# Key-value sums in five blocks instead of eight, and another order of VectorE's work in the value steps

## The chip, the cores and the metric

The kernel runs on one core of one Trainium2 chip. The metric is the device time of one execution in microseconds; lower is better. The time before is a median of 554.52 us over three runs (554.31 to 555.47).

## The reference, cut to what matters

A transformer block without a causal mask: a linear-attention layer and a token-mixing MLP, each after a layer norm, each with a residual. S = 2048 rows, D = 1024, 32 heads of 32. The change lies in the first half of the attention layer.

```python
h = layernorm(x)                                  # 2048 x 1024
q, k, v = split(h @ wqkv)                         # 32 heads of 32
phi = lambda t: where(t > 0, t + 1, exp(t)) + 1e-6
pq, pk = phi(q), phi(k)
kv = einsum("bhsd,bhse->bhde", pk, v)             # one 32 x 32 matrix per head, summed over all rows
z = einsum("bhsd->bhd", pk)
o = (pq @ kv) / (pq @ z + 1e-6)                   # then @ wo, the residual and the MLP
```

## The kernel before

The rows are worked in 16 tiles of 128, and from tile 2 on in pairs: pair q holds tiles 2q and 2q + 1. Each row tile is loaded (`load_x`), gets its statistics on VectorE (`ln_stats`), is normalised (`ln_finish`: two small ScalarE operations for `rstd`, one VectorE `tensor_scalar`, then a DMA transpose on the sync queue into `xnT`). The transposed rows are the matmuls' stationary operand.

Keys and values of a pair are two 256-row projections. Each is done by a Strassen-like scheme with seven products instead of eight (class `Run`, methods `p1` to `p7`). A product is four matmuls of 512 columns. The products need sums of blocks of the weights (`w_sums`, made once) and of the rows (`x_sums`, four VectorE subtractions or additions for each pair, into `xs`). The results are built up in three running PSUM tiles: `psA`, `psB`, `psC`, and `psE` for `p5`. ScalarE copies `psA` to `psB` and `psB` to `psC` between products. Two of the four output blocks are read by VectorE with an addition of `psE`'s copy (`add`, after `p7` from `psC` and after `p3` from `psB`); the two others are read by ScalarE (`evac`, after `p2` and `p4`). `p4` goes on accumulating in `psC` after the addition has read it.

A key step (`KRun`) sends its results through the feature map `phi`: ScalarE makes exp and relu, VectorE a `tensor_scalar` (line 190) and an addition (line 194), into a key buffer `pk`. A value step (`VRun`) writes its results into a value buffer `vaug`, which has a 33rd column of ones in every head, so that the sum over keys comes out with the matrix. `QRun` does the same for part of the queries, into `pqT`.

`run_step(n, prev, ...)` writes one step by hand, in program order (`pin`). It overlaps two runs: it issues `n.p1`, `prev.p3`, `prev.p4`, `n.p6`, `n.p2`, `n.p5`, `n.p7`, and between them the VectorE parts of both (`dve11` ... `dve22`: the four feature maps of a key pair) and callbacks (`after6`, `after5`, `after7`). Each engine runs its own instructions strictly in that order. The loop goes over q = 2 to 7 with a key step and a value step for each (K2, V2, K3, V3, ...); at q = 5 a query step follows each of them, and two query steps and the rest of the query projections follow the loop.

`kv_accum(i)` adds tile i to the key-value sums: 32 small matmuls, one for each head, with a stationary operand of 128 x 32 and a moving operand of 128 x 33. Four of them stand side by side in TensorE's columns (`tile_position`). It is called for two tiles at a time: tiles 0 and 1 before the loop, tiles 2q - 2 and 2q - 1 in every value step between `p5` and `p7`, and tiles 14 and 15 after the loop. That makes eight blocks of 64 matmuls. Keys and values stand in rings of four buffers each (`NPK`, `NVA`), which is two pairs.

In a value step before, VectorE's order from the statistics on is: the second feature map of the key step before it (`dve12`), the normalisation of a coming tile (`ln_finish` in `after5`), the addition after `p7`, the four sums for the next pair (`x_sums` in `after7`).

Of the kernel before, what the change touches and what calls it, by code (L numbers as in the profile page):

```python
# [10 lines left out]
P = 128  # L11
F32 = mybir.dt.float32
BF16 = mybir.dt.bfloat16
# [17 lines left out]
def kernel(  # L31
# [15 lines left out]
    S, D = x.shape  # L47
# [187 lines left out]
    class Inner:  # L235
        banks = 4
        behind = None
# [185 lines left out]
    class Mixer1(Product7):  # L423
# [27 lines left out]
        def finish(self):  # L451
            while self.todo:
                e = self.todo.pop(0)
                dve.tensor_tensor(e[:, CW:D], e[:, CW:D], e[:, 0:CW], ALU.subtract)
# [324 lines left out]
    with ExitStack() as actx:  # L779
# [13 lines left out]
        pqT = pqpool.tile([P, ND, S], BF16)  # L793
# [15 lines left out]
        with ExitStack() as a1:  # L809
            e1pool = a1.enter_context(tc.tile_pool(name="e1pool", bufs=1))  # L810
            epool = a1.enter_context(tc.tile_pool(name="epool", bufs=2))
            a1w = a1.enter_context(tc.tile_pool(name="a1w", bufs=1))
            wkv = a1w.tile([P, ND, 2 * D], BF16)
            NVA, NPK = 4, 4
            vaugs = [a1w.tile([P, ND * HB, DH + 1], BF16, name=f"vaug{t}") for t in range(NVA)]
            for t in range(NVA):
                nc.vector.memset(vaugs[t][:, :, DH:DH + 1], 1.0)
# [3 lines left out]

            def by_head(t):
                return t.rearrange("p (h e) -> p h e", e=DH)
            pks = [a1w.tile([P, D], BF16, name=f"pk{t}") for t in range(NPK)]
            tv = [
                t.bitcast(FP16).rearrange("p (k c) -> p k c", c=CW)
                for t in (wo_sb[:, 2 * t:2 * t + 2, :].rearrange("p a b -> p (a b)") for t in range(4))
# [50 lines left out]
            def ln_stats(i):  # L878
                ln[i] = ln_chunks(i, xs.pop(i))
                for c in range(NDC):  # L880
                    pin(ln[i][1](c))
                pin(ln[i][2]())

            def ln_finish(i):
                xn, _, _, scale, norm, _, _ = ln.pop(i)
                for op in scale():
                    pin(op)
                pin(norm(slice(0, D)))
                nc.sync.dma_start_transpose(out=xnT[:, :, i * P:(i + 1) * P], in_=xn[:])
# [29 lines left out]
            def kv_accum(i):  # L919
                for j in range(ND):  # L920
                    for q in range(HB):
                        h = j * HB + q
                        pin(nc.tensor.matmul(
                            kv_ps[q * DH:(q + 1) * DH, j, :],
                            lhsT=pks[i % NPK][:, h * DH:(h + 1) * DH],
                            rhs=vaugs[i % NVA][:, h, :],
                            start=False,
                            stop=(i == NS - 1),
                            skip_group_check=True,
                            tile_position=(0, q * DH),  # L930
                        ))

            hk2 = ND // 2

# [9 lines left out]
            def w_sums(mov, part):  # L944
                (b11, b12, b21, b22), (t1, t2, t3, t4) = mov
                for out, a, b in ((t1, b12, b11), (t2, b22, t1), (t3, b22, b12), (t4, b21, t2))[part]:
                    pin(nc.vector.tensor_tensor(out, a, b, ALU.subtract))
# [3 lines left out]
            def x_blocks(q):  # L951
                v = xnT[:, :, q * 2 * P:(q + 1) * 2 * P].rearrange("p (k two) (h f) -> p k two h f", two=2, h=2)
                return v[:, :, 0, 0, :], v[:, :, 1, 0, :], v[:, :, 0, 1, :], v[:, :, 1, 1, :]

            def x_sums(q, part=slice(0, 4), home=None):
                a11, a12, a21, a22 = x_blocks(q)
                s1, s2, s3, s4 = [xs_sb[:, q % 2, t] for t in range(4)] if home is None else home[q % 2]
                for out, a, b, op in (
                    (s1, a21, a22, ALU.add), (s2, s1, a11, ALU.subtract),
                    (s3, a11, a21, ALU.subtract), (s4, a12, s2, ALU.subtract),  # L960
                )[part]:
                    pin(nc.vector.tensor_tensor(out, a, b, op))  # L962
# [164 lines left out]
            def run_step(n, prev, after6=None, after5=None, after7=None, fill=None, after3=None):  # L1127
                if n is not None:
                    n.p1()
                else:  # L1130
                    fill()
                prev.late22()
                prev.p3()
                if after3 is not None:
                    after3()
                prev.dve22()
                prev.p4()
                if n is not None:
                    n.p6()
                prev.dve21()  # L1140
                if after6 is not None:
                    after6()
                if n is not None:
                    n.p2()
                    n.p5()
                prev.late12()
                if n is not None:
                    n.dve11()
                behind = QRun in (type(n), type(prev))
                if not behind:  # L1150
                    prev.dve12()
                if after5 is not None:
                    after5()
                if n is not None:
                    n.p7()
                if behind:
                    prev.dve12()
                if after7 is not None:
                    after7()
# [159 lines left out]
            NVP = NS // 2  # L1319
# [5 lines left out]
            def load_next(i):  # L1325
                if i < NS:
                    xs[i] = load_x(i)

            v1 = VRun(1)
            v1.p1()  # L1330
            q_fill()
            kv_accum(0)
            kv_accum(1)
            v1.p6()
            v1.p2()
# [9 lines left out]
            prev = v1  # L1345
# [3 lines left out]
            for q in range(2, NVP):  # L1349
                runs = [KRun(q), VRun(q)]  # L1350
                if q == 5:
                    runs = [runs[0], QRun(q // 2, 0), runs[1], QRun(q // 2, 1)]
                for n in runs:
                    kind = type(n).__name__[0]
                    i = {"K": 2 * q + 3, "V": 2 * q + 4}.get(kind, NS)
                    if q == 5 and kind == "Q":
                        i = NS - 1 if n.half == 1 else NS
                    elif q == 6 and kind == "K":
                        i = NS

                    def after6():
                        if i < NS:
                            ln_stats(i)

                    def after5():
                        if kind == "V":
                            kv_accum(2 * q - 2)
                            kv_accum(2 * q - 1)
                        if i < NS:
                            ln_finish(i)  # L1370
                            load_next(i + 2)

                    def after7():
                        if kind == "V" and q != 5 and q + 1 < NVP:
                            x_sums(q + 1)
                        if kind == "Q" and n.half == 1:
                            x_sums(q + 1, slice(0, 3))
                        if kind == "K" and q in q_sums:
                            w_sums(qmov, q_sums[q])
                        for x in late_sums.get((kind, q), ()):  # L1380
                            x_sums(x[0], x[1], late_parts)

                    def after3():
                        if type(prev) is QRun and prev.half == 1:
                            x_sums(q, slice(3, 4))

                    run_step(n, prev, after6, after5, after7, after3=after3)
                    prev = n
            r1, r2 = (QRun(1, half, late_home) for half in range(2))
# [3 lines left out]
            def last_accum():  # L1393
                kv_accum(NS - 2)
                kv_accum(NS - 1)

            run_step(r1, prev)
            run_step(r2, r1, after6=last_accum)
            run_step(None, r2, fill=q_fill)
            q_fill()  # L1400
# [472 lines left out]
```

## Time and profile before

| what | value |
|---|---|
| median of 3 runs (lowest, highest) | 554.52 us (554.31, 555.47) |
| the profiled execution, its span | 554.72 us, 553.0 us |
| PE busy | 546.5 us (99%), 3867 matmuls |
| DVE (VectorE) busy | 450.5 us (81%) |
| ACT (ScalarE) busy | 290.3 us (52%) |
| granted TensorE clock | 1.00 |
| small matmuls `kvps<-vaug,pk` | 512, first and last start at 33.6 and 140.9 us |

PE is TensorE's matmuls and PEld its weight loads, which overlap them; DVE is VectorE, ACT ScalarE, SP the sync queue. A row of the profile names the line of the code, the operation, what it writes and reads, and a bracket with the idle time before it and what ended it. Matmuls are pipelined, so that one's busy time runs into the next; how fast TensorE goes is read from the differences of the starts.

### The profile page before, as it was taken

To read this page: it belongs to the slowest core of one execution; us is meant where nothing else is said; L and a number is where in the kernel's file an instruction comes from. 1 tells how busy PE (TensorE), PEld (TensorE's weight loads), DVE (VectorE), ACT (ScalarE), POOL (GpSimd) and SP (SyncE) were. 2 spreads that over 40 slices of the span, in tenths; PEclk is the share of its full clock that TensorE was granted. 3 is DMA by queue.
4 is the path that set the end of the run, shared out by engine and by line. 5 is a ranking of instruction groups with operands and counts; after the bars stand their busy time and mean duration, and the time that the engine had idled before them with its cause. 6 is when DMAs were issued, how large, how long until landed. Compare 5 with 4: busy or idle time off the path is not lost.

```text
span 553.0 us, 9926 instructions
## 1 busy us (share of the span) xinstructions
PE 546.5 (99%) x3867; PEld 320.3 (58%) x3867; DVE 450.5 (81%) x875; ACT 290.3 (52%) x616; POOL 26.3 (5%) x36
## 2 busy tenths in 40 slices
PE   8999999999999999999999999999999999999997
PEld 3444446646634444456666766766445667667665
DVE  7798888765886999889988889888986979749747
ACT  5748768676788777636556465564210413413310
POOL 1000000000000000000000000000002103103111
PEclk9999999999999999999999999999999999999999
DMA  9933341205636991104041340422868749849334
GB/s 291 319 78 77 77 85 32 40 1 153 229 106 171 303 317 76 58 0 152 4 153 52 101 152 2 152 60 76 229 213 206 211 135 242 210 140 220 90 107 75
DMA packets 83087, 74.58 MB, mean 135 GB/s; under 512 B 15826, under 2 KB 74464, under 8 KB 83040
## 3 DMA queue, kind: packets, MB, share of 16 engines
q1 hardware_dynamic: 78656, 69.87, 42.5%
q0 software_dynamic: 4096, 3.68, 4.8%
q8 instruction: 30, 0.49, 0.4%
q10 hardware_dynamic: 288, 0.39, 0.2%
q14 instruction: 17, 0.14, 0.1%
HBM read 59.12 MB, written 11.67 MB: 128 GB/s over the span
## 4 chain that ended last, share of the span: by engine, by line
PE 96%; DMA 2%; DVE 1%; ACT 0%; issue 0%; SPq 0%; DVEq 0%; ACTq 0%
PE psI L230 26%; PE psC L230 16%; PE acc_t L230 13%; PE psB L230 8%; PE psC L973 4%; PE psB L973 4%; PE psA L973 4%; PE acc_t L893 3%; PE psB L342 2%; PE psA L342 2%; PE psE L973 2%; PE psC L342 2%; DMA wkv<-in_A_wqkv_dram 2%; PE acc_t L1308 2%; PE psA L1107 1%; PE psC L1107 1%
## 5 line engine op out<-in xcount | busy, mean ns | idle before, releaser
L230 PEld LDWEIGHTS <-is 128*128 128x128 f16 x736 | 71.9, 98 | 31.1 <-DVE hi L230 0.4
L230 PEld LDWEIGHTS <-sa 128*128 128x128 f16 x606 | 59.3, 98 | 27.1
L230 PEld LDWEIGHTS <-wq 128*128 128x128 bf16 (+1 forms) x496 | 48.5, 98 | 28.1 <-issue 1.0
L230 PE MATMUL acc_t<-wo_sb,pqT 128*128 128x512 f16 x256 | 55.6, 379 | 0.0
L487 POOL DMA_DIRECT2D out_dram<-wq x28 | 24.4, 935 | 514.6 <-DVE sa L334 395.7
L230 PEld LDWEIGHTS <-pqT 128*128 128x128 bf16 x256 | 25.0, 98 | 30.5 <-issue 0.6
L230 DVE TENSOR_TENSOR t<-psI,t 128x256 f32<-128x256 f32 (+1 forms) x45 | 20.8, 475 | 22.2 <-PE psI L230 20.9
L230 PE MATMUL psC<-gs,wq 128*128 128x512 f16 x140 | 34.1, 379 | 0.0
L973 PEld LDWEIGHTS <-xs 128*128 128x128 f16 x208 | 19.7, 98 | 22.1 <-DVE xs L962 0.8
L230 PE MATMUL psC<-hT,sa 128*128 128x512 f16 x112 | 31.2, 379 | 0.0
L230 PE MATMUL psI<-hi,is 128*128 128x256 f16 x200 | 30.0, 273 | 0.0
L230 PE MATMUL psB<-hT,sa 128*128 128x512 f16 x112 | 29.7, 379 | 0.0
L190 DVE TENSOR_SCALAR e_sb<-e_sb 128x512 bf16<-128x512 bf16 x64 | 18.4, 287 | 12.5 <-ACT e_sb L185 12.4
L230 DVE BATCH_NORM_STATS2 hst<-acc_t 128x6 f32<-128x512 f32 x32 | 21.2, 690 | 6.9 <-ACT h_bf L230 6.9
L973 PE MATMUL psA<-wkv,xnT 128*128 128x512 bf16 x104 | 26.7, 379 | 0.0
L973 PEld LDWEIGHTS <-xnT 128*128 128x128 bf16 x156 | 15.2, 98 | 18.7 <-issue 1.1
L230 ACT CAST h_bf<-acc_t 128x512 bf16<-128x512 f32 x32 | 18.4, 584 | 12.4 <-PE acc_t L230 12.2
L230 DVE TENSOR_TENSOR e<-psI,es 128x256 f32<-128x256 f32 x20 | 8.5, 425 | 19.9 <-PE psI L230 19.9
L230 PE MATMUL psC<-hT,wq 128*128 128x512 f16 x96 | 24.6, 379 | 0.0
L230 ACT COPY psI<-psI 128x256 f32<-128x256 f32 x50 | 18.0, 360 | 11.6 <-PE psI L230 9.7
L893 PE MATMUL acc_t<-wkv,xnT 128*128 128x512 bf16 x96 | 22.0, 379 | 0.8 <-DMA wkv<-in_A_wqkv_dram 0.6
L230 PE MATMUL psI<-gi,is 128*128 128x256 f16 x168 | 22.3, 273 | 0.0
(249 smaller groups left out, 1137.9 us busy)
## 6 DMA issues: line engine op xcount, KB each, us to landing
wq<-in_B_w_dram SPq DMA_DIRECT2D x14, 1024.0 KB, 7.7
gs<-parked SPq DMA_DIRECT2D x9, 896.0 KB, 4.8
wq<-in_B_w_dram SPq DMA_DIRECT2D x6, 896.0 KB, 8.5
wq<-in_B_w_dram SPq DMA_DIRECT2D x12, 448.0 KB, 6.3
shared_sb<-rd_dram SPq DMA_DIRECT2D x32, 128.0 KB, 3.9
out_dram<-h_bf SPq DMA_DIRECT2D x16, 256.0 KB, 3.6
x_sb<-in_A_x_dram SPq DMA_DIRECT2D x14, 256.0 KB, 3.0
w2o<-in_B_w_dram SPq DMA_DIRECT2D x4, 896.0 KB, 10.5
```

What stands on the lines that cost most here:

```text
L190: pin(nc.vector.tensor_scalar(e_sb[:], e_sb[:], 1.0, PHI_EPS, ALU.min, ALU.add))
L230: return (lambda *a, **kw: pin(op(*a, **kw))) if self.always or getattr(Held, self.key) else op
L342: pe.matmul(ps[:, cols], lhsT=lhs[:, k, :], rhs=mv(k)[:, cols], start=(start and k == 0), stop=(k == self.nk - 1), skip_group_check=True,)
L487: nc.gpsimd.dma_start(to, ot[:, a:b], accum_op=ALU.add)
L893: mm = nc.tensor.matmul(pp[:, 0:CW], lhsT=xnT[:, kt, i * P:(i + 1) * P], rhs=wkv[:, kt, c * CW:(c + 1) * CW], start=(kt == 0), stop=(kt == ...
L973: pin(nc.tensor.matmul(ps[:], lhsT=lhs[:, k, :], rhs=rhs[:, k, :], start=(start and k == 0), stop=(k == hk2 - 1), skip_group_check=True,))
L1107: pin(nc.tensor.matmul(out[:, j], lhsT=rhs[:, k, 2 * self.half + j, :], rhs=lhs[:, k], start=(start and j == 0 and k == 0), stop=(k == hk2 ...
L1308: nc.tensor.matmul(qp[:, 0:SW], lhsT=wq_sb[:, kt, j * P:(j + 1) * P], rhs=xnT[:, kt, u * SW:(u + 1) * SW], start=(kt == 0), stop=(kt == ND ...
```

## The change

There are six key buffers instead of four. The two new ones lie in a part of `pqT`, the tile of the queries' features, that isn't in use yet at that time (rows 4 and 5, first 1024 columns). The key-value sums of tiles 2 to 13 are no longer added in the value steps, two tiles at a time, but in the key steps q = 3, 5 and 7, four tiles at a time (pairs q - 2 and q - 1), again between `p5` and `p7`. With the first and the last block, that makes five.

In the value steps VectorE's order becomes: the addition after `p7`, the first two sums for the next pair, the second feature map of the key step before, the normalisation (with its transpose and the next load behind it on the sync queue), the other two sums. No instruction is added or removed on any engine.

```diff
-            NVA, NPK = 4, 4
+            NVA, NPK = 4, 6
...
-            pks = [a1w.tile([P, D], BF16, name=f"pk{t}") for t in range(NPK)]
+            pks = [a1w.tile([P, D], BF16, name=f"pk{t}") for t in range(4)] + [pqT[:, 4 + t, 0:D] for t in range(2)]
...
+            def kv_block(q):
+                for i in range(2 * q, 2 * q + 4):
+                    kv_accum(i)
...
                 if n is not None:
                     n.dve11()
-                behind = QRun in (type(n), type(prev))
+                behind = QRun in (type(n), type(prev)) or type(n) is VRun
                 if not behind:
                     prev.dve12()
                 if after5 is not None:
                     after5()
                 if n is not None:
                     n.p7()
-                if behind:
+                if behind and type(n) is not VRun:
                     prev.dve12()
                 if after7 is not None:
                     after7()
...
                     def after5():
-                        if kind == "V":
-                            kv_accum(2 * q - 2)
-                            kv_accum(2 * q - 1)
+                        if kind == "K" and q % 2 == 1:
+                            kv_block(q - 2)
+                        if kind != "V":
+                            finish()
+
+                    def finish():
                         if i < NS:
                             ln_finish(i)
                             load_next(i + 2)
 
                     def after7():
-                        if kind == "V" and q != 5 and q + 1 < NVP:
-                            x_sums(q + 1)
+                        if kind == "V":
+                            if q != 5 and q + 1 < NVP:
+                                x_sums(q + 1, slice(0, 2))
+                            prev.dve12()
+                            finish()
+                            if q != 5 and q + 1 < NVP:
+                                x_sums(q + 1, slice(2, 4))
```

## The prediction

> **What bounds the kernel now.** I read the page's chain that ended last first, then the waits of TensorE, then the stretch around one key-value block in order of time.
>
> ```profile
> PE 96%; DMA 2%; DVE 1%; ACT 0%; issue 0%; SPq 0%; DVEq 0%; ACTq 0%
> ```
>
> The end is set by TensorE nearly throughout. The waits of PE, over the whole span:
>
> ```profile
> PE acc_t L97 <- DVE m L105: 1.2, 1, 1.2
> PE acc_t L893 <- DMA wkv<-in_A_wqkv_dram: 0.6, 2, 0.3
> PE tp L1189 <- DVE xn L872: 0.5, 1, 0.5
> PE den_ps L230 <- DVE pqT L194: 0.2, 1, 0.2
> ```
>
> None lies in the projection stage (about 32 to 147 us) that the change touches. So the wait list alone says that nothing is to be had there. The order of time says otherwise, because a matmul that starts late by a tenth or two while the one before it drains is not listed as a wait. PE in the value step q = 2 and the start of key step 3 (start us, us busy):
>
> ```profile
> 51.57 1.03 PE L973 MATMUL psE<-wo_sb,xs 128*128 128x512 f16 x4
> 52.52 0.67 PE L923 MATMUL kvps<-vaug,pk 128*32 128x33 bf16 x64
> 53.12 1.04 PE L973 MATMUL psC<-wo_sb,xs 128*128 128x512 f16 x4
> 53.99 1.03 PE L973 MATMUL psA<-wkv,xnT 128*128 128x512 bf16 x4
> 54.86 1.03 PE L973 MATMUL psB<-wkv,xs 128*128 128x512 bf16 x4
> 55.91 1.02 PE L973 MATMUL psC<-wo_sb,xnT 128*128 128x512 f16 x4
> ```
>
> Read the differences of the starts, since the busy times overlap. A product of four 512-column matmuls takes 0.87 (53.12 to 53.99, 53.99 to 54.86). Two places are longer. From psE to the next psC there is 1.55, so the key-value block costs 1.55 - 0.87 = 0.68. And from psB to the last psC (step p4 of the values) there is 1.05, so 0.18 is lost. Who is late there is seen on VectorE:
>
> ```profile
> 53.78 0.29 DVE L190 TENSOR_SCALAR e_sb<-e_sb 128x512 bf16<-128x512 bf16 x1 [0.25 <-ACT e_sb L185]
> 54.30 0.42 DVE L194 TENSOR_TENSOR pk<-e_sb,r_sb 128x512 bf16<-128x512 bf16 x1 [0.22 <-ACT r_sb L187]
> 54.71 0.55 DVE L872 TENSOR_SCALAR xn<-x_sb,mv,rstd 128x1024 bf16<-128x1024 bf16 x1
> 55.17 0.69 DVE L1044 TENSOR_TENSOR vaug<-psC,e 128x512 bf16<-128x512 f32 x1
> 55.78 0.42 DVE L962 TENSOR_TENSOR xs<-xnT 128x512 f16<-128x512 bf16 x1
> ```
>
> p4 writes psC, so it has to wait for the addition that reads psC (L1044). That addition ends at 55.17 + 0.69 = 55.86 and p4 starts at 55.91. It could have begun near 54.25 (p7 has given its last matmul by 53.99, plus some 0.27 of drain, which is what an addition that nothing else delays shows: p7 over at 123.99, kt<-psC at 124.26). What stands ahead of it is the second feature map of the key step and the normalisation of the next rows.
>
> **Part one: fewer, longer blocks.** Eight blocks of 64 small matmuls become 64, 128, 128, 128, 64. The matmuls stay 512. What goes is three entries and three exits of the small-tile mode. The starts inside one block, in two windows that I cut after the 32nd start (us, PE busy with the instructions that overlap the window, load busy):
>
> ```profile
> 52.52:52.73 0.22, 0.21 (x32) 0.21 (x33) 1.00 0.00 0
> 52.73:53.01 0.28, 0.28 (x60) 0.28 (x42) 1.00 0.00 0
> ```
>
> The first 32 take 0.22, the next 32 start within 0.27 (the second count includes those still running). So 0.49 of the 0.68 is the work and about 0.20 is the change of mode, 0.09 in and 0.11 out. Eight blocks show this alike. If it were only that, three blocks fewer would give 3 x 0.20 = 0.60.
>
> But the pace inside the block is not even: 6.9 ns for each of the first 32 and 8.4 ns after that. I take it that the first 32 were standing ready behind the slow 512-column matmuls and the rest come as fast as they are handed out. Then a block of 128 has 32 quick ones and 96 slow ones: 0.20 + 0.22 + 96 x 0.0084 = 1.23, against 2 x 0.69 = 1.37 to 1.38 for two blocks. The gain is 0.15 for each merged block, 0.45 for three. The other bound is that every 64 again begin with 32 quick ones: 0.60. I take 0.45, as the row at hand for a matmul that follows 32 others is the slow one.
>
> [...] The trace's two windows disagree with an even pace, so the sum goes by them.
>
> **What the block's new place costs.** It moves from the value steps to the key steps q = 3, 5, 7, between p5 and p7, and covers the pairs q - 2 and q - 1. The newest inputs are the value tile of pair q - 1: its p3 addition on VectorE, and its p4 copy on ScalarE. Before, that p3 addition began at 57.24 and the key step's p5 ran from 58.50 to 59.36, where the block would start. So it has over 1 us to spare. The block's extra 1.2 us in the key step push p7 and its addition back, which only adds room for VectorE. The value step loses 0.68 in which VectorE could catch up. In the pair of 51.35 to 64.33 VectorE is busy for 11.52 of 12.98 us. With no block in either step, as in V3, K4, V4, a pair has 14 x 0.87 = 12.1, which still holds 11.5. Storage costs nothing: two of the six key buffers lie in a part of pqT that is written with queries only after the last block that reads them, and the operand form is the same.
>
> **Part two: addition and first sums ahead.** Counting from the end of p7 (T), by start-to-start steps of the rows: addition T+0.27, two sums T+0.87 and T+1.32, feature map T+1.66 and T+2.05, normalisation T+2.39, two sums T+2.85 and T+3.19, the p3 addition T+3.53, statistics after that. p4 is due at T+1.73 and the addition ends at T+0.96, so the wait of 0.18 is gone with 0.7 to spare. What is late next: p6 needs the second sum at T+2.6 and has it at T+1.75; p7 of the key step needs the third at T+5.2 and has it at T+3.3. The p3 addition frees psB and e5; the next copy into e5 comes after p5 at T+5.2. In the key step the normalisation waits for ScalarE's rstd (idle 0.48 before it at 60.73), and VectorE reaches it 0.2 before that, so the key addition still ends just before its p4 (61.19 + 0.68 = 61.87 against a start at 61.95). That is the thinnest cover: its margin is under 0.1, it is bare only in K4, and each tenth of lag beyond the 0.2 costs a tenth there. The sync queue: the value step's transpose and the x load behind it go out about 1.7 us later than now (normalisation at T+2.4 in place of T+0.7). Their readers are the sums of the next value step, some 10 us on; a transpose lands in 3.1 to 4.7. No cost. Q steps and V7 only change the order of work that has idle time around it.
>
> The wait stands in the value steps 2, 3, 4 (the same gap after 67.83 and 80.81, 1.06 each); V5 to V7 have none, and the one before the loop (p4 at 42.94, 0.09) isn't touched. So 3 x 0.19 = 0.57, with bounds of 0.3 (if lag eats half) and 0.6.
>
> **Sum.** 0.45 + 0.57 = 1.02 us. The profiled execution took 554.72 with a span of 553.0, 0.2 above the median of 554.52; the gain is the same on either. Nothing later is paced by anything but PE (the chain), so it is not given back: 554.52 - 1.02 = 553.50.
>
> **Rivals.** *The even pace*: merged blocks save 0.60, total 1.17, 553.35. For it: that a slower second half may belong to the second tile of each block, not to its length; against: I see nothing in that tile that differs. *The late normalisation bites*: VectorE lags, K4 waits, and part of the 0.57 stays: gain 0.4 to 0.8, 553.7 to 554.1. Against it are the margins above. *Slower by instruction supply*: a merged block is 128 matmuls and 128 loads in about a microsecond.
>
> ```profile
> q8 instruction: 30, 0.49, 0.4%
> ```
>
> The 3867 matmuls and as many loads come in 30 packets of 16 KB, about 258 instructions each, and 0.4% of 16 x 553 us is 1.2 us for a packet. A merged block eats a whole packet in the time of one transfer. Should PE have to stand until a packet lands, that is up to 1.2 in each of three blocks: 3.6 - 1.02, or 557.1. It decides from 0.34 of waiting per block. Against it: eight blocks of half a packet each must hold about four packet edges, and all take the same 0.66 or 0.67; and between blocks there are 20 us or more to fetch ahead. [...]
>
> **How the numbers follow.** Forecast 0.50, even pace 0.25, biting normalisation 0.14, instruction supply 0.11. A measurement of this kernel tells 0.2% from no change, that is 1.11 us. The forecast lies just inside it, so with the scatter of the runs (554.31 to 555.47) I give it 0.45 of coming out beyond; the even pace 0.9; together 0.45 for faster. The rest of these, and the third case, 0.44 for no difference; 0.11 slower. The range takes in the even pace with 0.4 of scatter, and reaches up to a gain of nothing and a little more: 552.9 to 554.8. Left out are most of the supply case and a few in a hundred below.
>
> **What would show it.** Right: three blocks of 128 that each cost 1.23 (start of psE to start of the next psC, less 0.87), with the second to fourth 32 at 8.4 ns; psB to psC of 0.87 in the steps V2 to V4; L1044 ahead of L190 and L872. Wrong: a hole inside a block near a packet of q8, a gap before the psC of key step 4's p4, or a pair without a block longer than 12.1 us.

## The result and the profile after

The changed kernel takes 553.34 us (median of 15 runs, 552.90 to 553.92) against 554.37 for the kernel before on the same chip (15 runs). The ratio is 0.9979, with a 95% interval of 0.9971 to 0.9987. That is 1.03 us less; 1.02 was forecast. The interval reaches from about 0.7 to 1.6 us, so that the two agree to the hundredth is luck. The profiled execution took 552.9, with a span of 551.1 us.

The spans of the two profiles differ by 1.9 us, and only part of that is the change's. The first product of the value step before the loop (psA) starts at 30.92 us before and at 30.17 after, though nothing was changed ahead of it. Over all profiles of this study it starts between 30.1 and 31.9. So I compare the **stage**: from that start to the start of the last key-value block, 140.41 - 30.92 = 109.49 before and 138.58 - 30.17 = 108.41 after. That is **1.08 less**. From the last block to the end both take 412.55.

The chain still lies on PE, and the waits of PE still name nothing in this stage (first lines of the page's chain, then all waits of PE):

```profile
PE 96%; DVE 1%; DMA 1%; issue 1%; ACT 0%; ACTq 0%; DVEq 0%
```

```profile
PE acc_t L97 <- DVE m L105: 1.2, 1, 1.2
PE tp L1193 <- DVE xn L872: 0.5, 2, 0.4
PE den_ps L230 <- DVE pqT L194: 0.2, 1, 0.2
PE acc_t L230 <- issue: 0.2, 1, 0.2
```

PE in order of time, value step 2 and key step 3 of the changed kernel (start us, us busy):

```profile
50.81 1.03 PE L977 MATMUL psE<-wo_sb,xs 128*128 128x512 f16 x4
51.67 1.03 PE L977 MATMUL psC<-wo_sb,xs 128*128 128x512 f16 x4
52.53 1.03 PE L977 MATMUL psA<-wkv,xnT 128*128 128x512 bf16 x4
53.40 1.03 PE L977 MATMUL psB<-wkv,xs 128*128 128x512 bf16 x4
54.26 1.03 PE L977 MATMUL psC<-wo_sb,xnT 128*128 128x512 f16 x4
...
56.85 1.03 PE L977 MATMUL psE<-shared_sb,xs 128*128 128x512 f16 x4
57.81 0.67 PE L923 MATMUL kvps<-vaug,pk 128*32 128x33 bf16 x64
58.30 0.71 PE L923 MATMUL kvps<-vaug,pqT 128*32 128x33 bf16 x64
58.94 1.04 PE L977 MATMUL psC<-shared_sb,xs 128*128 128x512 f16 x4
```

In the value step every start now stands 0.86 or 0.87 after the one before it; the 1.05 from psB to psC is gone. In the key step there are 2.09 us from psE to psC, so the block of 128 costs 2.09 - 0.87 = 1.22. VectorE in the same value step:

```profile
52.81 0.69 DVE L1048 TENSOR_TENSOR vaug<-psC,e 128x512 bf16<-128x512 f32 x1
53.41 0.41 DVE L966 TENSOR_TENSOR xs<-xnT 128x512 f16<-128x512 bf16 x1
53.86 0.42 DVE L966 TENSOR_TENSOR xs<-xs,xnT 128x512 f16<-128x512 f16 x1
54.20 0.29 DVE L190 TENSOR_SCALAR e_sb<-e_sb 128x512 bf16<-128x512 bf16 x1
54.60 0.42 DVE L194 TENSOR_TENSOR pqT<-e_sb,r_sb 128x512 bf16<-128x512 bf16 x1
54.94 0.54 DVE L872 TENSOR_SCALAR xn<-x_sb,mv,rstd 128x1024 bf16<-128x1024 bf16 x1
```

p7 has issued its last matmul by 52.53. The addition starts at T + 0.28 (T + 0.27 was worked out) and the normalisation at T + 2.41 (T + 2.39). VectorE was only just free for the addition in V2: the statistics (L865, 52.56, 0.21 us long) end 0.04 before it. The pace in the block, the small matmuls cut after every 32 starts:

```profile
57.80:58.02 0.23, 0.22 (x32) 0.22 (x33) 1.00 9.93 128
58.02:58.30 0.27, 0.27 (x59) 0.27 (x42) 1.00 0.35 2
58.30:58.56 0.27, 0.27 (x55) 0.27 (x44) 1.00 0.00 0
58.56:58.83 0.27, 0.27 (x53) 0.27 (x41) 1.00 0.06 5
```

The first 32 start within 0.22 us and each further 32 in 0.27. (The counts of the later windows include matmuls still running; the DMA columns at the end of the rows don't matter here.) The even pace is out.

### The profile page after: what moved, and what is told of

It reads as the page before. It is cut to its first block, busy times and chain, and to the rows that moved or that the text cites. A ratio compares the mean times of both kernels' runs of the same rounds, so it can differ in the third digit from the quotient of the medians.

```text
span 551.1 us, 9915 instructions
## 1 busy us (share of the span) xinstructions
PE 544.4 (99%) x3851; PEld 320.5 (58%) x3867; DVE 450.0 (82%) x875; ACT 289.9 (53%) x616; POOL 26.3 (5%) x36
## 4 chain that ended last, share of the span: by engine, by line
PE 96%; DVE 1%; DMA 1%; issue 1%; ACT 0%; ACTq 0%; DVEq 0%
PE psI L230 26%; PE psC L230 16%; PE acc_t L230 13%; PE psB L230 8%; PE psC L977 4%; PE psB L977 4%; PE psA L977 4%; PE acc_t L893 3%; PE psB L342 2%; PE psA L342 2%; PE psE L977 2%; PE psC L342 2%; PE acc_t L1312 2%; PE psA L1111 1%; PE psB L1111 1%; PE psC L1111 1%
```

## The experiments

Beside each total stands the length of the stage, to the hundredth from the trace's starts. A single run's total moves by up to 1.8 us with the start of the stage, so the stage decides wherever the two disagree. Lengths of waits and blocks are read from the starts, less 0.216 for each matmul of 512 columns, which is the usual distance of two such starts in these traces. V2 is the value step of pair 2, K4 the key step of pair 4, and so on.

### The blocks alone

The changed kernel with VectorE's order put back:

```diff
-                behind = QRun in (type(n), type(prev)) or type(n) is VRun
+                behind = QRun in (type(n), type(prev))
...
-                if behind and type(n) is not VRun:
+                if behind:
...
-                        if kind != "V":
-                            finish()
+                        finish()
```

and `x_sums(q + 1)` whole, after the addition.

> The five blocks alone; VectorE's order in the value steps is as before. Theory (each merged block saves one change of mode of 0.20 us, less 0.05 because its second half runs at the slower pace): three blocks of 1.22 to 1.23 us, the waits of 0.19 before the value step's p4 stay in V2 to V4, and perhaps shrink or grow as the value steps lose the block's 0.68 us in which VectorE caught up; projection stage shorter by 0.45, total about 553.9. If the missing 0.68 us falls on the late addition, the three waits grow to as much as 0.87 each and the merge alone is a loss of up to 1.6 us, about 556.0. Rival (even pace): 0.60 saved, 553.75.

Measured: 556.73 us, ratio 1.0048 (1.0036 to 1.0061). The stage is 112.16, which is 2.67 longer than before. The blocks of 128 cost 1.22 as they should. But the waits of PE now name the addition:

```profile
PE psC L977 <- DVE vaug L1048: 2.8, 6, 0.7
```

Six waits, and by the starts they are 0.90 in each of V2, V3, V4 and 0.35 to 0.37 in V5, V6, V7, where there was none. The balance: three merges save 3 x 0.157 = 0.47; V2 to V4 lose 3 x (0.896 - 0.193) = 2.11 more and V5 to V7 1.07. That makes +2.71; +2.67 was measured. So not the gain of my first theory but the upper of my two outcomes for the waits, 0.87, came about true, and the three more in V5 to V7 I had not listed, so that the total is 0.7 above the 556.0 that I had for it. Half of the change alone is a loss, by the totals as by the stage.

### The order alone

The changed kernel with the blocks put back, two tiles in every value step, on four key buffers:

```diff
-            NVA, NPK = 4, 6
+            NVA, NPK = 4, 4
...
-                        if kind == "K" and q % 2 == 1:
-                            kv_block(q - 2)
+                        if kind == "V":
+                            kv_accum(2 * q - 2)
+                            kv_accum(2 * q - 1)
```

> VectorE's new order alone; eight blocks on four key buffers. Theory (the addition ahead ends 0.7 us before p4 is due): the three waits of 0.19 go, the blocks cost 0.69 each as before, gain 0.57, total about 553.8. Rival (the merged blocks are what frees VectorE, the order alone brings a new wait in the key steps through the later normalisation): gain 0 to 0.3, with a gap before the p4 of K3 or K4.

Measured: 553.67 us, ratio 0.9991 (0.9982 to 1.0). The interval touches no change, so the total alone doesn't settle it. The stage is 108.92, which is 0.57 shorter, as forecast. In the value step of this kernel psB and p4's psC stand 0.86 apart:

```profile
54.25 1.03 PE L977 MATMUL psB<-wkv,xs 128*128 128x512 bf16 x4
55.11 1.03 PE L977 MATMUL psC<-wo_sb,xnT 128*128 128x512 f16 x4
```

So the new order is worth 0.57 without the blocks, the blocks are worth -2.67 without the order, and both together are worth 1.08. With the order in place, merging adds 0.51.

### The blocks moved, none merged

The kernel before, with its blocks of 64 in the key steps:

```diff
                     def after5():
-                        if kind == "V":
+                        if kind == "K":
                             kv_accum(2 * q - 2)
                             kv_accum(2 * q - 1)
```

> The kernel before, with its blocks of 64 (tiles 2q - 2 and 2q - 1) moved from the value step to the key step of the same q, none merged; VectorE's order as before. Theory (the block between a value step's p5 and p7 was cover for the late addition, whose start is set by ScalarE's exp after the copy of psE): the waits before the value's p4 grow as with the five blocks alone, to 0.9 in V2 to V4 and 0.36 in V5 to V7, the blocks cost what they did, stage longer by 3.2, total about 557.4. Rival (the key step's block gives VectorE its time back): the waits stay under 0.3, total within 0.5 of before. Rival (it was the merging that cost): nothing changes.

Measured: 558.06 us, ratio 1.0069 (1.0052 to 1.0085). The stage is 112.65, 3.16 longer (3.2 expected, with the sizes of the waits taken over from the blocks alone). The six waits are the same as with the blocks alone, 0.89 to 0.90 three times and 0.35 to 0.37 three times, and the blocks cost what they did before. So the loss belongs to the place of the block, not to its length. Room in the key step gave VectorE nothing back. The wait of 0.90 in V2, as this kernel's PE shows it:

```profile
54.58 1.03 PE L973 MATMUL psB<-wkv,xs 128*128 128x512 bf16 x4
56.34 1.02 PE L973 MATMUL psC<-wo_sb,xnT 128*128 128x512 f16 x4 [0.73 <-DVE vaug L1044]
```

Why the room doesn't help can be seen in the rows of VectorE shown before the change: the feature map ahead of the addition is itself held by ScalarE's exp and relu (idle 0.25 and 0.22). ScalarE makes these behind the copy of psE, that is after p5 of the same step. With a block between p5 and p7 that chain ran beside the block; without it, it sticks out by the length of the block. The starts in V2 bear this out: from psE to the addition there are 3.60 us before (51.57 to 55.17), 3.61 with the blocks alone (50.89 to 54.50) and 3.61 here (51.99 to 55.60). The chain keeps its length, and only p7 and p4 come sooner. In V5, where the feature map isn't ahead of the addition, the normalisation is held by ScalarE's rstd, which stands behind the same copy.

### Every block cut in two

The kernel before, tile 2q - 1 moved behind p7:

```diff
                             kv_accum(2 * q - 2)
-                            kv_accum(2 * q - 1)
...
                     def after7():
+                        if kind == "V":
+                            kv_accum(2 * q - 1)
```

> The kernel before, with every block of the loop cut in two: tile 2q - 2 between p5 and p7 of the value step, tile 2q - 1 after its p7. Fourteen blocks instead of eight, the same matmuls. Theory (the quick first 32 stand ready behind slow matmuls): each block of 32 costs 0.20 + 0.22 = 0.42, the second tile too runs at 6.9 ns, and each cut costs 0.15; projection stage longer by 0.9, less what the waits before p4 shrink because p4 comes 0.42 later than p7 ends (three times up to 0.19). Rival (the second tile of a block is slow in itself): its 32 take 0.27, and each cut costs 0.20, 1.2 in all, less the same.

Measured once: 554.6 us in all; the stage is 109.89, 0.40 longer than before. The second tile, now with a product ahead of it, runs at the quick pace (small matmuls of this kernel, 32 starts):

```profile
53.27:53.49 0.22, 0.21 (x32) 0.22 (x32) 1.00 0.26 74
```

A block of 32 costs 0.41 by the starts, so a cut costs 2 x 0.41 - 0.69 = 0.13 (0.15 expected), or about 0.80 for six; the waits in V2 to V4 fell from 0.19 to 0.06, 0.39 in all. That leaves 0.41, near the 0.40. The second tile isn't slow in itself.

### The two tiles interleaved

```diff
-                for j in range(ND):
+                if i % 2 == 0:
+                    return
+                for j, i in ((j, t) for j in range(ND) for t in (i - 1, i)):
```

> The kernel before, with the two tiles of each block interleaved by head group (four matmuls of one tile, four of the other, to the same sums). Theory (place in the block sets the pace): as before, the first 32 in 0.22, the next in 0.27, 0.69 a block, no change of time. Rival (the second tile is slow, by its operands or because it adds to sums written just before): an uneven pace of fours through the whole block, or a slower block, 0.75 or more.

Measured once: the total of 555.68 is that of a late start (31.88); the stage is 109.49, the same as before to the hundredth. The small matmuls again change pace after the 32nd (the second column is VectorE's here, not the loads'):

```profile
53.47:53.69 0.22, 0.21 (x32) 0.00 (x0) 1.00 0.00 0
53.69:53.96 0.27, 0.27 (x60) 0.00 (x0) 1.00 0.00 0
```

So the place in the block sets the pace, not the operands. That the first 32 stand ready behind the 512-column matmuls was my estimate from the two paces; no run here shows what holds them.

### The long blocks done twice

```diff
-                for i in range(2 * q, 2 * q + 4):
+                for i in [*range(2 * q, 2 * q + 4)] * 2:
                     kv_accum(i)
```

> The changed kernel, with each of the three long blocks done twice, so 256 matmuls (512 instructions) in a row, whose sums count these tiles double. Theory (hand-over pace, nothing runs dry): each block costs 0.20 + 0.22 + 224 x 0.0084 = 2.30, that is 1.08 more than 1.22, and the kernel is 3.2 us longer than the changed one. Rival (instruction supply, a packet of 256 instructions in 1.2 us): a hole in each block, up to 1.2 more each, 3.2 to 7 us longer. Rival (quick ones every 64): 0.98 more each, 2.9.

Measured once: 561.73 us; the stage is 117.27, 8.86 longer than the changed kernel's. 3.2 of it is the work, and the sum is beyond the 7 at which my rival's range ended. The rest are holes, one large one in each block of 256 (the waits of PE, then the second block):

```profile
PE kvps L923 <- issue: 5.1, 3, 2.4
```

```profile
84.97 1.48 PE L923 MATMUL kvps<-vaug,pk 128*32 128x33 bf16 x162
88.76 0.91 PE L923 MATMUL kvps<-vaug,pk 128*32 128x33 bf16 x94 [2.30 <-issue]
```

After 162 matmuls PE stands for 2.5 us from start to start, with nothing to wait for that the profile shows. In this stretch one 16 KB packet of the instruction queue goes out at 86.12 and takes 1.08 us; PE goes on at 88.76. The three blocks stop after 146, 162 and 193 matmuls, for 0.65, 2.49 and 2.55 us, and the first again briefly (0.13) near its end. In the first and the third block the packet starts at 57.39 and 127.77, so that of the three one starts 1.5 us before the stop and two within 0.2 us of it; PE goes on 1.2 to 1.6 us after the packet has ended. So the rows point to the supply of instructions, though no run changed the supply alone. I had put a hole at up to 1.2 us; the longest here is 2.55. At 128 there is none: no pair of starts within a block is over 0.03 apart.

### A later VectorE in the value steps

The changed kernel, the fourth sum made three times in V2 to V4:

```diff
                                 x_sums(q + 1, slice(2, 4))
+                            if q < 5:
+                                x_sums(q + 1, slice(3, 4))
+                                x_sums(q + 1, slice(3, 4))
```

> The changed kernel, with the fourth sum done two more times in the value steps 2 to 4 (the same values again), so VectorE is 0.67 us later from the value's p3 addition on. Theory (0.2 of slack in front of the normalisation of a key step, and none behind it; a key step with a block has room): one wait of 0.4 to 0.47 before the p4 of K4 (which stands in V4), none for K3 and K5, total 0.4 above the changed kernel. Rival (VectorE carries its lag on through V4): also a wait before the value's p4, 0.8 or more in all. Rival (there is more slack than I read): no wait.

Measured once: 554.1 us; the stage is 109.00, 0.59 longer than the changed kernel's. There is one wait, before the p4 of K4 (in V4), of 0.59:

```profile
74.49 1.02 PE L977 MATMUL psC<-pqT,xnT 128*128 128x512 f16 x4 [0.43 <-DVE kt L1071]
```

The place is as expected; the size isn't. The two repeated sums put the p3 addition off by 0.92, counted from the stage's start, and not by 0.67 (0.46 for each; unrepeated sums start 0.33 apart). 0.92 less 0.59 is 0.3 of room, of which the changed kernel shows 0.21 as idle time before K4's normalisation:

```profile
72.40 0.55 DVE L872 TENSOR_SCALAR xn<-x_sb,mv,rstd 128x1024 bf16<-128x1024 bf16 x1 [0.21 <-ACT rstd L869]
```

### Towards a faster version: the step before the loop

The value step before the loop still waits 0.09 for its addition. Three kernels, all from the changed one. First, the addition ahead of the sums and the statistics:

```diff
-            x_sums(2)
-            ln_stats(G0 + 2)
             v1.p5()
             v1.p7()
+            x_sums(2)
+            ln_stats(G0 + 2)
```

> The changed kernel with the same order of addition and sums for the value step before the loop too. Theory: the 0.09 us before its p4 goes, nothing else moves: 0.09 under the changed kernel, about 553.25. Rival: the sums for pair 2 and the statistics come later and K2 waits for them: nothing gained.

Measured: 553.77 us, ratio 0.9995 (0.9986 to 1.0003); the stage is 108.97, 0.56 longer than the changed kernel's. The 0.09 is gone, but K2's p6 stands 0.65 late, and not for VectorE's sums. ScalarE in this kernel:

```profile
42.78 0.29 ACT L868 ACTIVATE lnv<-mv,eps_ln 128x1 f32<-128x1 f32 x1 [0.88 <-DVE mv L865]
43.11 0.20 ACT L869 ACTIVATE rstd<-lnv 128x1 f32<-128x1 f32 x1
43.22 0.58 ACT L990 COPY psB<-psA 128x512 f32<-128x512 f32 x1
```

The copy to psB, which p6 needs, stands behind the logarithm, and that waits for the statistics that I had pushed back. My rival had K2 wait for the sums or the statistics, but not by way of ScalarE's copy, and not at a loss of 0.56. So the statistics went ahead of the sums:

```diff
             v1.p7()
-            x_sums(2)
             ln_stats(G0 + 2)
+            x_sums(2)
```

> The changed kernel with, in the value step before the loop, the addition first, then the next tile's statistics, then the sums for pair 2. Theory (in the run with the sums ahead of the statistics, ScalarE's copy of psA to psB stood behind the logarithm that waits for these statistics): statistics done by 41.2, the copy is in time for K2's p6, the 0.09 before the first p4 goes; 0.09 under the changed kernel. Rival: the sums are now too late for K2's p6, a wait there of 0.1 to 0.5.

Measured: 553.11 us, ratio 0.9979 (0.9970 to 0.9987); the stage is 108.33, 0.08 under the changed kernel's. And with the first block merged into K3's as well (`kv_accum(0)` and `kv_accum(1)` dropped from the step before the loop, `kv_block` over tiles 0 to 5, two more key and two more value buffers in `pqT`), first in the order of the first of these kernels, then in that of the second:

> As the run before, and the first block is merged too: tiles 0 to 5 in one block of 192 in K3, then 128, 128, 64, on eight key buffers and six value buffers, the additional ones in parts of the queries' tile. Theory: another 0.15 saved, the block of 192 costs 0.20 + 0.22 + 160 x 0.0084 = 1.77; total about 553.1, a gain of 1.25 on before. Rival (a long block outruns the supply of instructions, 384 in 1.8 us): a hole of up to 1.2 inside the block, about 554.2.

> The same, with the first block merged into that of K3 (blocks of 192, 128, 128, 64). Theory (the mode change saved is the gain): 0.15 less again, 0.24 under the changed kernel. Rival (between 33 and 46 us VectorE is busy 12.6 of 13.2 us and TensorE, 0.69 sooner there, only waits for it): the wait appears before K2's p6 or V2's p4, no gain or up to 0.4 lost. The block of 192 costs 1.76 as in the run before.

The first took 554.1 us, ratio 1.0003 (0.9994 to 1.0012); the stage is 109.00, 0.59 longer than the changed kernel's. The same wait of K2's p6 is 0.85 there, 0.20 longer, with the block of 0.69 gone from the time ahead of it. The second took 553.25, ratio 0.9984 (0.9974 to 0.9994); the stage is 108.16, 0.25 under the changed kernel's, as the sum had it (0.24). The block of 192 costs 1.76 in both, with no hole. Yet its total isn't lower. From the last block to the end the two profiles with four blocks take 412.84 and 412.85, 0.3 more than the 412.55 of the others, in a single gap near 315 us, in the MLP, that the list of waits doesn't name. The run with the lagging VectorE has a gap of that size too, near 379 us. What makes it stays open. The changed kernel itself, measured beside the statistics first and the second kernel with four blocks:

> The changed kernel itself, to stand beside the two before it on the same chip: 1.0 under before.

553.17 us, ratio 0.9982 (0.9973 to 0.9991); the stage is 108.41, as in its first profile. So the second kernel with four blocks has the shortest stage, but together with what follows it the statistics first are the best (520.88 against 521.00, with 520.94 and 520.97 for the changed kernel's two profiles), and by the totals the changed kernel, the one with the statistics first and the second with four blocks can't be told apart.

## Why the prediction was right, and where it was thin

**The merge** was 0.15 a block from the two paces, 0.45 in all. The blocks cost 1.223 against 2 x 0.690, so 0.157 each and 0.47 in all. The choice of the slow row for matmuls 33 to 128 was right, and the cutting and the interleaving show that it is the place in the block that counts.

**The waits** were 3 x 0.19 = 0.57; the order alone gives 0.57, and the times from T on are met within 0.02.

**The sum** was 1.02; the stage gives 1.08, the medians 1.03. It was passed on whole, since 412.55 us follow in both. Of the 0.06, 0.02 is the merge and 0.01 the waits, which are 0.193 each by the unrounded starts; the other 0.02 to 0.03 I can't place.

**What was thin** is the step on the block's new place. It said that the value step loses 0.68 us in which VectorE could catch up and went on to count the busy time of a pair, 11.5 in 12.1, as if that settled it. It doesn't: with the old order VectorE has the same work, and yet 3.2 us are lost (the moved blocks). The cover was for one chain, p5, copy of psE, exp, feature map, normalisation, addition, and not for a sum of work. The forecast came out because in part two's order the addition no longer stands behind that chain: it waits for p7 and the statistics alone, so the cover wasn't needed any more. The working didn't put it so, and didn't ask whether the statistics end in time once p7 comes 0.68 sooner; in V2 they do by 0.04, which is luck. And the two terms were written as if they added, and alone they are -2.67 and +0.57. The price of the cover, should it be gone, ought to have stood beside the merge: 0.70 more on three waits and some 0.36 on three new ones.

**The rivals.** The even pace fell by the windows (0.22 us for the first 32 starts, 0.27 for each 32 after them). The late normalisation did not bite; its place and about its slack (0.2 read, 0.3 found) are shown by the lag. The supply of instructions cost nothing at 128 matmuls (1.22 a block) nor at 192 (1.76, against 1.77 worked out), and most likely made the holes at 256. Length alone doesn't tell: a block of 256 first stopped after 146 matmuls, fewer than the 192 that ran through, so presumably it also counts where in a packet the block begins; no run varied that. The fetch of a 16 KB packet starts 1.5 us before one of the stops and within 0.2 us of the two others, and the time lost was 0.65 to 2.55 us. How far ahead of the engine instructions are fetched no run here shows.

## What to carry to other kernels

A short burst of work on the bounding engine can be the cover of a late chain elsewhere: here it was a block of 0.69 us, and moving the blocks lost 3.16. Before it is moved, time the chain that runs beside it, from the event that starts it, with the burst gone; a busy share for the pair of steps doesn't show this. Two edits that touch the same cover must be summed together, since one of them alone may be a loss larger than the gain of both (here 2.67 against 1.08). Read start-to-start times on TensorE: the waits of 0.19 here stood in no list of waits, and one of 0.90 is listed as 0.73.

## What the runs showed of the hardware

- Column-tiled matmuls of 128 x 32 by 33 columns, in the blocks before and after the change, start within 0.22 us for the first 32 and 0.27 for each further 32. After 512-column matmuls, a block costs another 0.09 us on the way in and 0.11 on the way out.
- 512 small matmuls and loads in a row stopped in all three places tried, after 146, 162 and 193 matmuls, for 0.65, 2.49 and 2.55 us, near the fetch of a packet of instructions; 256 in a row (every block of 128 matmuls in these profiles) and 384 (two blocks) ran through.
- The start of the stage moved by 1.8 us between profiles of kernels that are alike up to there (30.1 to 31.9), more than the whole effect. A stage cut out of the trace repeated to 0.01 us (108.41 and 108.41 for the changed kernel, 109.49 and 109.49 for the one before and its interleaved form).
